# The entry to the last stage of a backward pass: one more block turned on TensorE, four row transfers moved to GpSimd's queue, new places for the stage's tiles

## The chip, the cores and the metric

The kernel runs on one core of one Trainium2 chip. Five engines work side by side, each with its own instruction stream: TensorE (PE, matrix products and transposes), VectorE (DVE), ScalarE (ACT), GpSimd (POOL) and SyncE (SP, which here only starts transfers). Transfers between HBM and SBUF, or inside SBUF, are done by 16 DMA engines; an engine's instruction stream only issues them. The metric is device time in microseconds (us) for one execution. The median over three runs is 2489.8 us.

## The reference

The reference is the forward pass of one transformer block and its gradients:

```
h = layernorm(x) * (1 + ca) + sa
x = x + ga * attention(h, wqkv, wo)          # 32 heads of 16, S = 2048, D = 512
h = layernorm(x) * (1 + cb) + sb
x = x + gb * (square(relu(h @ w1 + b1)) @ w2 + b2)
(sa, ca, ga, sb, cb, gb) = split(silu(c) @ w_mod, 6)
out, vjp = jax.vjp(f, x, wqkv, wo, w1, b1, w2, b2, c, w_mod); grads = vjp(grad_out)
```

Outputs are the block's result and the gradients of x, wqkv, wo, w1, b1, w2, b2, c and w_mod, all in bf16.

## The kernel before

The forward pass and the gradients of the dense part take the first 1,100 us or so. What matters here are the two last stages.

**The attention gradient** (lines 1541 to 1774) treats the 32 heads as eight head groups (`hg`) of four. One *unit* is one tile of 128 queries against 512 keys for the four heads of a group; there are NU = 512 of them. For each unit, TensorE makes the scores (`score`), ACT the exponentials (`expo`), TensorE the products with the upstream gradient and DVE the score gradients `dS_u` (`dp_pair`). Four units with neighbouring query tiles form a *block* `b`; there are 128. The gradient of Q needs `dS_u` turned, keys on partitions, and the turned data of a block is gathered in one tile, `dsT`, of which there are three in rotation. There are two ways to turn a unit:

- by a transposing DMA that SP issues (`transpose_unit`; line 1631 turns two units at once, line 1629 a single one);
- by 16 TensorE transposes (`pe_turn`, eight to a half, into the PSUM tile `ptT`) and a copy out of PSUM (token `T`, line 1760).

In even blocks all four units go by DMA, in two transfers of two. In odd blocks units 0 and 1 go together by DMA (line 1631), unit 2 alone by DMA (line 1629) and unit 3 over TensorE. Then `dq_quad` (line 1681, 16 matrix products for a block into the PSUM tile `dqacc`) and `dq_out` follow: ACT scales the result into `dqtmp` (line 1694) and POOL adds it to `dQacc` (line 1699); in the last round over the keys the sum goes to `dQst` in bf16. Two lists of tokens, `order_t` and `order_n`, fix by hand the order of instructions on PE, ACT, DVE, SP and POOL. `dq_out` of block b stands two blocks after its scores, so that the last two blocks' Q gradients are finished behind the last score.

**The last stage** (lines 1776 to 1959) takes the gradients of Q (`dq`, four slices of 128 rows) and of K and V (`vk`, eight slices), each slice 128 rows by 2048 tokens, and makes from them

- `dh1`: for each of 16 token tiles, 12 matrix products with `wT` (line 1858) into `pdh1`, then the layer norm's backward on DVE and ACT (lines 1862 to 1883) with `x0J` and `dx1J`, and the gradient of x;
- row sums of the same tiles (line 1877);
- `dwqkv`: 12 blocks of the weight gradient (`b` = 0 for Q, 1 and 2 for K and V; four `ic` each), 16 matrix products each with `h1J` (line 1892), then one or two copies out of PSUM and a store; beside them the gradients of w_mod and c (`wmod_grad`, `c_grad`, `c_out`).

`dwqkv` needs `dq` and `vk` with tokens on partitions, so at the stage's start every slice is turned by TensorE (line 1918, 24 groups of eight transposes) and copied to `dq_tok` or `dvk_tok` by DVE (line 1924) or ACT (line 1926), in the order of the list `order`.

Some of the slices are in SBUF at that point. Five are not: SP loads four (line 1778) into the buffers of the head group just finished and half of a fifth (line 1779), then `wT` (line 1781, 1.5 MB), and then copies the last head group's Q gradient from `dQst` into the other half of that fifth slice with four transfers of 16 rows (line 1783). Then come `x0J` and `dx1J` (lines 1792 and 1794, two token tiles to a transfer) and `sums_bc` (line 1799, 1.5 MB written). All of these stand on SP's one queue, in this order, and each waits where it stands. The transfers of that queue signal on eight semaphores in turn, so an issue can also wait for the transfer eight places ahead of it.

The stage's tiles are in a pool `big`, whose space is handed out in the order of allocation and lies over the buffers of the stage before. A tile's first writer therefore waits for the last user of what lay there. `wT` and the small tile `nb1` (line 1786, the first instruction of the stage on DVE) lie over the `dsT` tile of the last block and wait for its `dq_quad`.

At the end of `dwqkv`, step 9 of 0 to 11 calls `c_out`: two small DVE instructions form `dc` (lines 1837 and 1838), TensorE turns it (line 1840), ACT copies it and SP stores it. For `b` > 0, ACT copies one half of a weight block and DVE the other (lines 1903 and 1905), into one tile, and one transfer stores both (line 1907).

## Time and profile before

| what | value |
|---|---|
| median of three runs (2485.82 to 2491.23) | 2489.8 us |
| the profiled execution's span | 2501.3 us |
| attention gradient's last score gradient on DVE ends | 2378.1 us |
| first product of `dh1` starts | 2404.5 us |
| first product of `dwqkv` starts | 2454.1 us |
| last product of `dwqkv` ends | 2497.6 us |
| PE busy over the span | 93% |
| ACT, DVE, POOL busy over the span | 92%, 73%, 20% |

Times are from the start of the span of one profiled execution. The profile names an instruction by engine, line and operation with output and inputs; "idle before" is how long the engine stood still in front of it and what ended that. SPq is SP's instruction stream: its duration is that of issuing a transfer, not of the transfer. PE runs at a granted clock that the profile gives as a share of full speed. A wait for several things is put down to the one that came last by the profile; which one that is has at times to be worked out.

### The profile page before, as it was taken

The numbers are of one execution on the slowest core, as the hardware profiler recorded it, in microseconds if no ns is written. First come the engines' busy times: TensorE is split into PE (matmuls) and PEld (weight loads), VectorE is DVE, ScalarE is ACT, GpSimd is POOL, SyncE is SP. The second block draws the span as 40 slices with busy tenths as digits, with TensorE's granted clock in tenths as the row PEclk, the third lists the DMA queues.
The fourth block names the chain that finished last, engine by engine and source line by source line (L and its number), as shares of the span: only waits on it lengthen the run. The fifth ranks groups of instructions, "written<-read, shape, count | busy, mean of one in ns | idle before, by whom it ended". The sixth has DMA issues, their size and how long they took to land.

```text
span 2501.3 us, 49888 instructions
## 1 busy us (share of the span) xinstructions
PE 2324.0 (93%) x18948; PEld 783.4 (31%) x19036; DVE 1837.7 (73%) x2377; ACT 2303.7 (92%) x3560; POOL 488.0 (20%) x661
## 2 busy tenths in 40 slices
PE   8899899989998998999999999999999999999989
PEld 3232233223332333443223323233232323332344
DVE  6555354455435444579989999999999999999965
ACT  7999999999998999539999999999999999999944
POOL 2111223323533453110111101111011110110100
PEclk9999999999998999999999999999999999999999
DMA  4468463258546865979999999999999999999984
GB/s 146 130 167 176 144 150 97 88 166 142 98 95 142 151 131 110 256 200 196 201 192 206 199 198 202 196 204 203 205 205 198 205 202 199 200 198 214 201 253 133
DMA packets 1189503, 437.70 MB, mean 175 GB/s; under 512 B 1065867, under 2 KB 1160521, under 8 KB 1188878
## 3 DMA queue, kind: packets, MB, share of 16 engines
q1 hardware_dynamic: 1152414, 389.35, 79.0%
q0 software_dynamic: 19872, 27.09, 6.5%
q10 hardware_dynamic: 16976, 18.07, 2.9%
q8 instruction: 149, 2.44, 0.4%
q14 instruction: 92, 0.75, 0.1%
HBM read 98.30 MB, written 70.80 MB: 68 GB/s over the span
## 4 chain that ended last, share of the span: by engine, by line
ACT 40%; PE 38%; issue 8%; DVE 7%; DMA 3%; SPq 1%; ACTq 1%; POOL 0%; DVEq 0%; another core or an unknown queue 0%; POOLq 0%
ACT E_u L1600 24%; ACT ET L578 12%; PE dqacc L1681 4%; PE psST L576 3%; PE psS_A L1594 3%; PE accVK L1654 2%; PE pm L233 2%; ACT dsT L1760 2%; PE psS_B L1594 2%; PE pdh L1858 2%; PE oacc L592 2%; PE psS_C L1594 2%; PE pwq L1892 2%; PE pm L500 2%; PE pm L410 2%
## 5 line engine op out<-in xcount | busy, mean ns | idle before, releaser
L1616 DVE TENSOR_TENSOR dS_u<-psD_u,E_u 128x1024 bf16<-128x1024 f32 x1024 | 1185.9, 1218 | 77.1 <-PE psD_u L1614 30.2
L578 ACT ACTIVATE ET<-psST 128x1024 bf16<-128x1024 f32 x1024 | 941.9, 1242 | 16.6 <-PE psST L576 16.3
L1600 ACT ACTIVATE E_u<-psS_A 128x512 bf16<-128x512 f32 x768 | 509.9, 664 | 10.8 <-PE psS_C L1594 8.5
L1600 ACT ACTIVATE E_u<-psS_B 128x512 bf16<-128x512 f32 x768 | 503.2, 655 | 10.8 <-DMA dsT<-dS_u 2.7
L1614 PE MATMUL psD_u<-iv,ido 32*128 32x512 bf16 x2048 | 409.1, 388 | 1.5 <-DVE dS_u L1616 1.3
L576 PE MATMUL psST<-qt_sb,kt_sb 32*128 32x512 bf16 x2048 | 313.8, 386 | 48.0 <-ACT ET L578 41.0
L1600 ACT ACTIVATE E_u<-psS_C 128x512 bf16<-128x512 f32 x512 | 334.3, 653 | 3.1 <-PE psS_B L1594 1.1
L1594 PE MATMUL psS_B<-ik,iq 32*128 32x512 bf16 x768 | 296.1, 386 | 11.7 <-ACT E_u L1600 4.4
L1594 PE MATMUL psS_A<-ik,iq 32*128 32x512 bf16 x768 | 294.5, 383 | 11.0 <-DVE dwlast L237 1.0
L1699 POOL TENSOR_TENSOR dQacc<-dQacc,dqtmp 128x512 f32<-128x512 f32 x64 | 81.2, 1268 | 858.8 <-ACT dqtmp L1694 797.4
L1594 PEld LDWEIGHTS <-iq 32*128 32x128 bf16 x2048 | 129.7, 91 | 313.9 <-issue 296.9
L1654 PE MATMUL accVK<-dS_u,qz 128*32 128x512 bf16 x2048 | 213.5, 388 | 0.5 <-PE psD_u L1614 0.2
L592 PE MATMUL oacc<-ET,vaug 128*32 128x512 bf16 x2048 | 207.0, 394 | 3.9 <-DVE ostage L596 3.9
L1663 PE MATMUL accVK<-E_u,dOs_tok 128*16 128x512 bf16 x2048 | 204.5, 388 | 0.0
L1594 PE MATMUL psS_C<-ik,iq 32*128 32x512 bf16 x512 | 194.2, 379 | 4.5
L576 PEld LDWEIGHTS <-kt_sb 32*128 32x128 bf16 x2048 | 84.3, 91 | 328.2 <-issue 306.5
L1681 PE MATMUL dqacc<-dsT,KS_tok 128*32 128x512 bf16 x2048 | 145.7, 382 | 18.8 <-DMA dsT<-dS_u 5.0
L1760 ACT ACTIVATE dsT<-ptT 128x1024 bf16<-128x1024 bf16 x128 | 144.1, 1126 | 13.1 <-PE ptT L1644 12.2
L251 DVE COPY part<-pm 128x512 f32<-128x512 f32 (+2 forms) x106 | 65.2, 615 | 121.9 <-PE pm L233 111.8
L1614 PEld LDWEIGHTS <-ido 32*128 32x128 bf16 x2048 | 105.2, 91 | 101.3 <-issue 94.9
L1654 PEld LDWEIGHTS <-qz 128*32 128x32 bf16 x2048 | 58.5, 94 | 178.0 <-issue 162.9
L1699 POOL TENSOR_TENSOR dQst<-dQacc,dqtmp 128x512 bf16<-128x512 f32 x32 | 40.6, 1270 | 266.1 <-ACT dqtmp L1694 266.1
(415 smaller groups left out, 2688.7 us busy)
## 6 DMA issues: line engine op xcount, KB each, us to landing
p_st<-part POOLq DMA_DIRECT2D x36, 256.0 KB, 4.6
kt_sb<-qkT_st POOLq DMA_DIRECT2D x124, 64.0 KB, 3.0
wA<-in_B_w_dram SPq DMA_DIRECT2D x28, 256.0 KB
wB<-w1T_st SPq DMA_DIRECT2D x21, 256.0 KB
wA<-w2T_st SPq DMA_DIRECT2D x21, 256.0 KB
wB<-in_B_w_dram SPq DMA_DIRECT2D x21, 256.0 KB
p_st<-part POOLq DMA_DIRECT2D x28, 192.0 KB, 4.6
p_st<-part SPq DMA_DIRECT2D x18, 256.0 KB
```

The costliest lines, as they stand in the source:

```text
L576: PE.matmul(ps[:, hi, :], kt_sb[r:r + 32, kt * P:(kt + 1) * P], qt_sb[r:r + 32, :], start=True, stop=True, tile_position=(r, 0))
L578: ACT.activation(ET[:, 2 * pair:2 * pair + 2, :], ps[:], AF.Exp, scale=SCALE)
L592: PE.matmul(oacc[32 * hq:32 * hq + 32, :], lhsT, ET[:, hq, :], start=(kt == 0), stop=(kt == TT - 1), tile_position=(0, 32 * hq), skip_grou ...
L1594: PE.matmul(psS[:], st["q"][r:r + 32, qt * P:(qt + 1) * P], st["k"][r:r + 32, kc * 512:kc * 512 + 512], start=True, stop=True, tile_positi ...
L1600: ACT.activation(bst[u][0][:, hq, :], sst.pop((u, hq))[:], AF.Exp, scale=SCALE)
L1614: PE.matmul(psD[:, hi, :], st["do"][r:r + 32, qt * P:(qt + 1) * P], st["v"][r:r + 32, kc * 512:kc * 512 + 512], start=True, stop=True, til ...
L1616: DVE.tensor_tensor(dS_u[:, 2 * pair:2 * pair + 2, :], psD[:], E_u[:, 2 * pair:2 * pair + 2, :], ALU.mult)
L1654: PE.matmul(cur["vk"][32 * hq:32 * hq + 32, :], hst[hg]["qz"][:, qt, hq, :], bst[u][1][:, hq, :], start=(qt == 0), stop=False, tile_positi ...
L1663: PE.matmul(acc[32 * hq:32 * hq + DH, :], dOs_tok[:, qt, (hg * 4 + hq) * DH:(hg * 4 + hq + 1) * DH], E_u[:, hq, :], start=False, stop=(qt ...
L1681: PE.matmul(acc[32 * hq:32 * hq + 32, :], KS_tok[:, kc * 4 + kt, h * DH:h * DH + 32], tT[:, :, hq * 4 + kt, :], start=(kt == 0), stop=(kt ...
L1699: POOL.tensor_tensor(dst2, dst, tmp[:], ALU.add)
L1760: ACT.activation(dst, pt[:], AF.Identity)
```

## The change

The change touches the end of the attention gradient and the last stage.

- The third unit of the last block (unit 510) is turned by TensorE: `last_turn`, 16 more transposes into two PSUM banks that the scores had, each half copied by ACT. SP's single-unit transfer for it is dropped. The copies for unit 511 (token `T` of the last block) go from ACT to DVE.
- The four transfers `dQst` to `xs["dq", 3]` are issued by POOL and no longer by SP.
- `order` begins with the four slices of the idle head buffers and has ("vk", 6) later.
- `sums`, `dmod` are allocated ahead of `wT`, `dvk_tok` is two tiles of layout [4, TT, P] where it was one of [TT, HG, P], with the three `wmodJ` buffers as tiles of their own around them, `nb1` is allocated later, and its computation stands behind the transposes.
- The load of `sums` moves behind the loads of `x0J` and `dx1J` for six token tiles.
- `c_out` is split: `c_sum` (the two DVE instructions) stays at step 9 of `dwqkv`, the rest moves to step 10.
- For `b` > 0, the two halves of a weight block get a tile and a store each.

```
 def transpose_unit(u):
     if on_pe(u // 4) and qi >= 2:
-        if qi == 2:
+        if qi == 2 and u < NU - 2:
             SP.dma_start(out=dqt[u // 4][:, qi], in_=bst[u][1]..., transpose=True)
...
+def last_turn(half):
+    pt = psx.tile([P, 8, P], BF, name="ptL", tag=("ps0", "ps1")[half])
+    for i in range(8):
+        kt = i % 4
+        PE.transpose(pt[:, i, :], held["last"][:, 2 * half + i // 4, kt * P:(kt + 1) * P], identb[:])
+    ACT.activation(dqt[NU // 4 - 1][:, 2, 8 * half:8 * half + 8, :], pt[:], AF.Identity)
...
     elif c == "t" and 0 <= b - 1 < NU // 4:
+        if b == NU // 4:
+            last_turn(i - 1)
         pe_turn(b - 1, i - 1)
     elif c == "T" and 0 <= b - 1 < NU // 4:
         dst, pt = held.pop(i - 1)
-        ACT.activation(dst, pt[:], AF.Identity)
+        if b == NU // 4:
+            DVE.tensor_copy(dst, pt[:])
+        else:
+            ACT.activation(dst, pt[:], AF.Identity)
...
+sums = big.tile([P, 6, D], F32, name="sums_bc")
+dmod = big.tile([P, 6, D], BF, name="dmod_bc")
 wT = big.tile([P, 12, D], BF, name="wT_all")
 SP.dma_start(out=wT[:], in_=wT_st...)
 for h in range(4):
-    SP.dma_start(out=xs["dq", 3][64 + DH * h:64 + DH * h + DH, :], in_=dq_last[32 * h:32 * h + DH, :])
-order = (("vk", 6), ("vk", 0), ("vk", 1), ("vk", 2), ("vk", 3), ("dq", 0), ("vk", 7), ...)
-nb1 = big.tile([P, TT], F32, name="nb1")
-DVE.scalar_tensor_tensor(out=nb1[:], in0=mean1[:], scalar=-1.0, in1=rstd1[:], ...)
+    POOL.dma_start(out=xs["dq", 3][64 + DH * h:64 + DH * h + DH, :], in_=dq_last[32 * h:32 * h + DH, :])
+order = (("vk", 0), ("vk", 1), ("vk", 2), ("vk", 3), ("dq", 0), ("vk", 6), ("vk", 7), ...)
 load_x(0)
 load_x(1)
-sums = big.tile([P, 6, D], F32, name="sums_bc")
-SP.dma_start(out=sums[:], in_=rows_st[2:8, :]...)
-dmod = big.tile([P, 6, D], BF, name="dmod_bc")
+wmod_tile()
+wmod_tile()
+dvk_tok = [big.tile([P, 4, TT, P], BF, name=f"dvk_tok{i}") for i in range(2)]
+wmod_tile()
+nb1 = big.tile([P, TT], F32, name="nb1")
...
-PE.matmul(pw[:], h1J[:, t, ic * P:(ic + 1) * P], rhs[:, t, :], ...)
+PE.matmul(pw[:], h1J[:, t, ic * P:(ic + 1) * P], dq_tok[:, t, :] if b == 0 else dvk_tok[b - 1][:, :, t, :], ...)
...
     for i in range(2):
+        wblk = wk.tile([P, D], BF, name="wqblk", tag=("prod1", "dxn1")[i], bufs=3)
         ...
-    SP.dma_start(out=dst, in_=wblk.rearrange("p (v c) -> p v c", v=2))
+        SP.dma_start(out=rows[:, c0:c0 + 256], in_=wblk[:, 0:256])
...
+DVE.scalar_tensor_tensor(out=nb1[:], ...)          # behind the 24 groups of transposes
 norm_tile(0)
 for t in range(TT):
+    if t == 2:
+        SP.dma_start(out=sums[:], in_=rows_st[2:8, :]...)
...
     if i == 2 * DC + 1:
+        c_sum()
+    if i == 2 * DC + 2:
         c_out()
```

In the changed program, PE's order behind the last score is: `last_turn` and `pe_turn` by halves, the rest of the K and V products, `dq_quad` of block 126, ten transposes of the last stage, `dq_quad` of block 127, and then the other transposes. The first copy into `dvk_tok` on DVE and the load of `wT` both still wait for `dq_quad` of block 127, since they lie over its `dsT`.

More of the change, by code (lines that the diff above doesn't have):

```diff
@@ L1618, in dp_pair @@
                 held["dS"] = dS_u
+            if u == NU - 2:
+                held["last"] = dS_u
         def on_pe(b):
@@ L1782 @@
         for h in range(4):
-            SP.dma_start(out=xs["dq", 3][64 + DH * h:64 + DH * h + DH, :], in_=dq_last[32 * h:32 * h + DH, :])
-        order = (("vk", 6), ("vk", 0), ("vk", 1), ("vk", 2), ("vk", 3), ("dq", 0), ("vk", 7), ("dq", 1), ("vk", 4), ("dq", 2), ("vk", 5), ("dq", 3))
-        nb1 = big.tile([P, TT], F32, name="nb1")
-        DVE.scalar_tensor_tensor(out=nb1[:], in0=mean1[:], scalar=-1.0, in1=rstd1[:], op0=ALU.mult, op1=ALU.mult)
+            POOL.dma_start(out=xs["dq", 3][64 + DH * h:64 + DH * h + DH, :], in_=dq_last[32 * h:32 * h + DH, :])
+        order = (("vk", 0), ("vk", 1), ("vk", 2), ("vk", 3), ("dq", 0), ("vk", 6), ("vk", 7), ("dq", 1), ("vk", 4), ("dq", 2), ("vk", 5), ("dq", 3))
         x0s, dx1s = {}, {}
@@ L1797, with wmod_tile @@
         load_x(1)
-        sums = big.tile([P, 6, D], F32, name="sums_bc")
-        SP.dma_start(out=sums[:], in_=rows_st[2:8, :].unsqueeze(0).to_broadcast([P, 6, D]))
-        dmod = big.tile([P, 6, D], BF, name="dmod_bc")
-        wms = {}
+        wms, wtags = {}, ["wmodJ0", "wmodJ1", "wmodJ2"]
+        def wmod_tile():
+            wtags.append(wtags.pop(0))
+            return big.tile([P, 3 * D], BF, name="wmodJ", tag=wtags[-1], bufs=1)
+        wmod_tile()
[3 more added lines that the diff above has]
+        nb1 = big.tile([P, TT], F32, name="nb1")
         def load_wmod(k, h):
-            wms[k, h] = big.tile([P, 3 * D], BF, name="wmodJ", tag="wmodJ", bufs=3)
+            wms[k, h] = wmod_tile()
             SP.dma_start(out=wms[k, h][:], in_=w_mod[k * P:(k + 1) * P, 3 * D * h:3 * D * h + 3 * D])
@@ L1833, in c_grad, with c_sum, c_out @@
                                      scale=1.0, scalar=0.0, op0=ALU.mult, op1=ALU.add, accum_out=ccols[:, k, h:h + 1])
-        def c_out():
-            dc = wk.tile([P, 4], F32, name="dc", bufs=1)
+        dc = wk.tile([P, 4], F32, name="dc", bufs=1)
+        def c_sum():
             DVE.tensor_tensor(dc[:].unsqueeze(2), ccols[:, :, 0:1], ccols[:, :, 1:2], ALU.add)
             DVE.tensor_tensor(dc[:], dc[:], colc[:, 4:8], ALU.mult)
+        def c_out():
             pc = psd.tile([P, D], F32, name="pdc", tag="pdh1")
@@ L1845 @@
         dq_tok = dpool.tile([P, TT, D], BF, name="dq_tok", tag="dt")
-        dvk_tok = big.tile([P, TT, HG, P], BF, name="dvk_tok")
         xns = {}
@@ L1888, in dwqkv @@
         def dwqkv(b, ic):
-            rhs = dq_tok if b == 0 else dvk_tok[:, :, 4 * (b - 1):4 * b, :].rearrange("p t g c -> p t (g c)")
             pw = psw.tile([P, D], F32, name="pwq", tag="pw")
             for t in range(TT):
-                PE.matmul(pw[:], h1J[:, t, ic * P:(ic + 1) * P], rhs[:, t, :], start=(t == 0), stop=(t == TT - 1))
-            wblk = wk.tile([P, D], BF, name="wqblk", tag="prod1", bufs=3)
+                PE.matmul(pw[:], h1J[:, t, ic * P:(ic + 1) * P], dq_tok[:, t, :] if b == 0 else dvk_tok[b - 1][:, :, t, :], start=(t == 0), stop=(t == TT - 1))
             rows = out_2[ic * P:(ic + 1) * P, :]
             if b == 0:
+                wblk = wk.tile([P, D], BF, name="wqblk", tag="prod1", bufs=3)
                 ACT.activation(wblk[:], pw[:], AF.Identity)
@@ L1900, in dwqkv @@
                     srcv = pw.rearrange("p (g v d) -> p g v d", v=2, d=DH)[:, :, 1 - i, :]
-                    dstv = wblk[:, i * 256:(i + 1) * 256].rearrange("p (g d) -> p g d", d=DH)
+                    wblk = wk.tile([P, D], BF, name="wqblk", tag=("prod1", "dxn1")[i], bufs=3)
+                    dstv = wblk[:, 0:256].rearrange("p (g d) -> p g d", d=DH)
                     if i == 0:
@@ L1905, in dwqkv @@
                         DVE.tensor_copy(dstv, srcv)
-                dst = rows[:, D:3 * D].rearrange("p (v c) -> p v c", v=2)[:, :, (b - 1) * 256:b * 256]
-                SP.dma_start(out=dst, in_=wblk.rearrange("p (v c) -> p v c", v=2))
+                    c0 = D * (1 + i) + (b - 1) * 256
+                    SP.dma_start(out=rows[:, c0:c0 + 256], in_=wblk[:, 0:256])
         with tc.manual_schedule(engines={PE.engine, ACT.engine, DVE.engine}):
@@ L1921 @@
                     else:
-                        dst = dvk_tok[:, 8 * g:8 * g + 8, i, :]
+                        dst = dvk_tok[i // 4][:, i % 4, 8 * g:8 * g + 8, :]
                     if (2 * k + g) % 3 != 1:
@@ L1926 @@
                         ACT.activation(dst, pt[:], AF.Identity)
+            DVE.scalar_tensor_tensor(out=nb1[:], in0=mean1[:], scalar=-1.0, in1=rstd1[:], op0=ALU.mult, op1=ALU.mult)
             norm_tile(0)
@@ L1932 @@
                     load_x(t // 2 + 2)
+                if t == 2:
+                    SP.dma_start(out=sums[:], in_=rows_st[2:8, :].unsqueeze(0).to_broadcast([P, 6, D]))
                 if t in (4, 6, 7):
```

## The prediction

> **What bounds the kernel now.** I read the clock and span of the core, the chain of waits in order of time from 2376 us on, the timeline of each engine there, SP's own waits, stretches by engine and clock, and last the end. Up to 2376 us nothing is changed but line numbers; all that can move lies behind it. The chain first (start, duration, what):

> ```profile
> 2378.12 3.91 SPq L1631
> 2382.07 1.93 SPq L1629
> 2384.06 1.04 SPq L1778
> ...
> 2386.64 9.24 DMA qz<-dQc
> 2395.90 6.92 DMA x0J<-in_A_x_dram
> 2402.84 1.01 PE ptq L1918 x8
> ```

> From the last score gradient to PE's last transposes the chain is SP and transfers alone: SP is held by issuing two transposing DMAs, then loads follow. The last chain entry names x0J, but PE at 2402.84 transposes the slice `dq` 3, whose rows come by line 1783. The timeline (start, duration, instruction, idle before):

> ```profile
> 2386.60 1.17 PE L1681 MATMUL dqacc<-dsT,KS_tok 128*32 128x512 bf16 x16 [4.35 <-DMA dsT<-dS_u]
> 2387.84 0.38 SPq L1781 DMA_DIRECT2D wT_all<-wT_st  x1
> 2387.88 0.18 DVE L1786 SCALAR_TENSOR_TENSOR nb<-mean,rstd 128x16 f32<-128x16 f32 x1 [9.77 <-PE dqacc L1681]
> 2389.84 3.80 SPq L1783 DMA_DIRECT2D qz<-dQst  x4
> 2402.84 1.01 PE L1918 MATMUL ptq<-identb,qz 128*128 128x128 bf16 x8 [4.74 <-DMA x0J<-in_A_x_dram]
> 2404.50 0.63 PE L1858 MATMUL pdh<-wT_all,vkb 128*128 128x512 bf16 x1
> ```

> Everything waits for the last block's `dqacc` (4.35 us, for the single-unit transpose): wT's load, the first copies of DVE, and the rows of dQst. Those rows are issued behind wT on the same queue. SP's own waits say when wT was there:

> ```profile
> SPq L1794 <- DMA wT_all<-wT_st: 5.1, 1, 5.1
> SPq L1781 <- PE dqacc L1681: 0.5, 1, 0.5
> ```

> The 5.1 us ended at SP's issue at 2401.41, so wT landed at 2401.40; the trace's semaphore counts put the four row transfers at 2400.15 to 2402.38, the transpose of line 1631 at 2383.96 and that of line 1629 at 2386.47. So two arrivals a microsecond apart set the start of `dh1`: wT, then the rows, then 16 transposes (2402.84 to 2404.50). From there PE has no gap over a microsecond until step 9 of `dwqkv`:

> ```profile
> 2468.33 20.88 PE L1892 MATMUL pwq<-dvk_tok,h1J 128*128 128x512 bf16 x94
> 2490.41 0.27 PE L1840 MATMUL pdc<-identf,dc 128*4 128x128 f32 x1 [1.20 <-DVE dc L1838]
> 2490.52 7.07 PE L1892 MATMUL pwq<-dvk_tok,h1J 128*128 128x512 bf16 x31
> ```

> **The change part by part.**

> *SP without line 1629.* SP issues the first load at 2382.07 where it was 2384.06: 1.99 us earlier. Its waits (last scores at 2376.6, last K products at 2380.1) are over by then. What lands before `dqacc` of block 127 is now line 1631's transfer, 2383.96 against 2386.47: 2.51 us earlier.

> *The 16 transposes and the copies.* A group of eight takes 0.62 us on PE (line 1644), so 1.2 us more; out of the same stretch go 19 transposes of line 1918, by `order`, which ran there. ACT's copies 2 x 1.02 us (line 1760) are now those of unit 510, and DVE copies unit 511 after its last score gradient, at 2378.1: two copies of 0.69 (line 1924) with eight transposes between, done at about 2380.3, where ACT was done at 2380.43. `dqacc` of block 126 (2380.48, 1.05 us) does not move, and ends 2.4 us ahead of the landing. I cost this at nothing; the cover is that wait, and without it the 1.2 us would show.

> *`dqacc` of block 127* runs 2384.1 to 2385.2 (0.13 us after the landing, as before; before it ended at 2387.77). wT's issue follows at 2385.3, behind five loads whose issuing takes 2382.07 to 2384.65. POOL's sum (line 1699, 1.27 us from 2388.55) was done 2.05 us after `dqacc`: now 2387.2.

> *wT.* SP starts its loads 1.99 us earlier and the queue is free of line 1629's data 2.51 us earlier, so wT lands 2398.9 to 2399.4. Against that the rows, 0.26 MB, now go beside it: at the 241 GB/s of the stretch 2398.1 to 2402.8 at most 1.1 us. I take 2399.8 (bounds 2398.9 and 2400.5).

> *The rows on POOL's queue.* POOL has nothing behind them but the end of the program. Issues of 64 KB cost POOL 0.49 us in the median and 1.16 at most (line 188), so the last starts at about 2388.7 to 2390.7. The median time to landing (last number) over the run:

> ```profile
> kt_sb<-qkT_st POOLq DMA_DIRECT2D x124, 64.0 KB, 3.0
> ```

> and in the loaded stretch 918.5 to 924.5, with the load of SP's and ACT's queue above it:

> ```profile
> q1 hardware_dynamic: 1570, 1.88, 94.7%
> ...
> kt_sb<-qkT_st POOLq DMA_DIRECT2D x2, 64.0 KB, 4.1
> ```

> So 4.1 us beside a nearly full queue; the longest of 124 took 10.1. So the rows are there at 2392 to 2395, at worst about 2400.8. The 22 groups of transposes and copies ahead of them took 2387.97 to 2398.98, bound by the copies; from 2385.2 that ends near 2396.3, and the last slice is turned by 2397.5. All this is 2 us ahead of wT, which alone then sets the start of `dh1`: about 2399.9 for 2404.50, a gain of 4.6 us (bounds 5.5 and 3.9).

> *The clock.* PE's two waits cost half speed afterwards (stretch, length, busy us by engine, clock, DMA share, GB/s):

> ```profile
> 2398.10:2402.80 4.70, 0.00 (x1) 0.00 (x0) 0.88 (x2) 0.17 (x1) 0.00 (x0) 0.81 1.03 241
> 2402.80:2408.00 5.20, 4.94 (x24) 2.97 (x26) 0.69 (x1) 2.43 (x3) 0.00 (x0) 0.51 0.93 349
> ```

> The half clock lasted until 2407.9, so 3.4 us of `dh1` ran at half speed and lost 1.7 us. Afterwards PE would idle some 2.4 us ahead of wT. In this trace the idle times of 2.3 us (764.6, 1776.0) and 2.85 us (792.2) were each followed by half clock too, in stretches of 3.41 or 6.83 us. I take the same 1.7 us, so no difference; bounds 1.7 us gained (no half clock) and 1.7 lost (6.83 us of it). [...]

> *c_sum and c_out.* PE's last product before the stall started at 2468.33 + 20.88 - 0.38 = 2488.83; the pitch is 0.216 us, so the next was due at 2489.05 and came at 2490.52: 1.47 us. With `dc` ready a step earlier only the transpose's 0.11 us (2490.41 to 2490.52) stays: 1.4 us gained. The DVE instructions follow the same copy as before and now have 3.4 us of cover. Bounds 1.2 (the stall alone) and 1.5.

> *Stores of halves, layouts, `order`, sums, `nb1`.* The last store goes out after DVE's half either way; it is half as large, and ACT's half is issued (0.38 us) while DVE copies (0.42). I take 0.1 us gained, bounds 0.4 lost (an issue in the way) and 0.3 gained. A product reading `dvk_tok` in four pieces has the shape of `dqacc`'s reads of dsT, 382 ns against 388 for whole rows: nothing. `nb1` (0.18 us) is needed only by `norm_tile` once x0J is there, and x0J is next behind wT. Sums, first used at 2457, lands by 2415.

> Sum: 4.6 + 0 + 1.4 + 0.1 = 6.1 us; span 2501.3 to 2495.2. The profiled span lies 11.5 us over the median of the runs; the stages are the same, so I take the gain off the median: 2489.8 - 6.1 = 2483.7.

> **Rivals.**

> *The rows come last (15%).* DVE copies back to back from 2385.3 to 2396.3, and POOL must prepare its transfers in that time. If it could do so only afterwards, the last would be issued at 2397.8 and land 4.1 us later; 0.46 us and 16 transposes (1.66) give `dh1` at 2404.0, gain 0.5 + 1.5: 2487.8. Against it: of 124 issues of this size none took over 1.16 us, in a part of the run where DVE was 30 to 70% busy, with copies out of PSUM among its work. [...]

> *Warm entry (12%).* wT finds PE at full clock: 1.7 us more, 2482.0.

> *wT comes no earlier (6%).* If the 16 engines, not the issues, set 2401.40, only the rows' way is shortened: `dh1` at 2401.5, gain 3.0 + 1.5: 2485.3. For it: the engines are 97% busy or more from 2386.6 to 2402.8. Against: 2.5 us of transposing data leave that queue.

> *Slower (7%).* POOL's queue is served only when SP's is empty. SP now puts wT, six x0J and dx1J and sums in front: 2.4 + 1.6 + 1.6 + 1.6 = 7.1 MB from 2384 at 263 to 300 GB/s, done at 2408 to 2411. The rows land then, `dh1` starts 2.1 us later at 2410 to 2413, and 6 to 8 us lost against 1.5 gained give 2494 to 2497. It decides from a landing after 2403.9 on. Against it is the 4.1 us at 94.7% load.

> **How the numbers follow.** My forecast has 60%, with a range of its own of 2481.5 to 2486 from the bounds above. The predicted time is 2483.7. With the rivals and some 2 us for the median of few runs I give 2480.5 to 2489.5. A measurement of this kernel tells about 0.2% (5 us) from no change, so 2484.8 is the edge: of the forecast three quarters lie below it and of the warm entry nearly all, with a little of the others 0.57 faster; 0.35 the same; 0.08 slower.

> **What would show it.** SP's first load at 2382.1; `dqacc` of block 127 at 2384.1; POOL's four transfers landed by 2395 and the last transposes done by 2398 without a wait over a microsecond; `dh1` waiting for wT and starting near 2399.9; half clock for some 3.4 us of it; no idle PE at line 1864. It is wrong if `dq` 3 is the slice that PE waits for, or if wT lands later than 2401.

## The result, and the profile after

The changed kernel took 2482.47 us (median of 22 runs, 2471.86 to 2493.62), the kernel before 2490.35 us (22 runs, 2478.20 to 2499.89). The ratio is 0.9968, its 95% interval 0.9954 to 0.9981: some 7.9 us, a third of a per cent, faster. The forecast was 2483.7.

The profiled executions differ by more: 2501.3 us before, 2482.6 after. The last score gradient on DVE, ahead of which only line numbers changed, ended at 2378.11 before and at 2367.11 after. So 11.0 of the 18.7 us are no work of the change (the last section says what goes with part of them), and 7.7 us lie behind that point. From here on, times called *marks* are counted from the end of the last score gradient.

The chain of waits after (start, duration, what) answers to the chain of before:

```profile
2366.00 8.22 DMA dsT<-dS_u
2374.22 0.04 issue
2374.27 1.86 PE dqacc L1690 x16
2376.13 0.02 SPq L1797
...
2376.18 12.50 DMA wT_all<-wT_st
2388.68 0.05 issue
2388.73 0.39 PE pdh L1881
```

But for 0.02 us ahead of wT, SP's issuing no longer stands in it. What stands there is the last transposing transfer, `dqacc` of block 127, wT's load and `dh1`. The timeline after (start, duration, instruction, idle before and who ended it):

```profile
2370.93 0.58 SPq L1792 DMA_DIRECT2D iq<-dQc  x1
...
2374.27 1.84 PE L1690 MATMUL dqacc<-dsT,KS_tok 128*32 128x512 bf16 x16 [3.31 <-DMA dsT<-dS_u]
...
2376.18 0.38 SPq L1797 DMA_DIRECT2D wT_all<-wT_st  x1
...
2378.45 2.07 POOL L1799 DMA_DIRECT2D qz<-dQst  x4 [0.30 <-POOL dQst L1708]
...
2387.29 0.61 PE L1941 MATMUL ptq<-identb,qz 128*128 128x128 bf16 x8 [1.05 <-DVE dvk_tok L1947]
...
2388.73 0.39 PE L1881 MATMUL pdh<-wT_all,iq 128*128 128x512 bf16 x1 [0.38 <-DMA wT_all<-wT_st]
```

`dh1` waits for wT, as forecast, but only by 0.38 us. PE's wait ahead of slice `dq` 3 shrank from 4.74 to 1.05 us. Its releaser is named as a DVE copy; by the trace's semaphore counts the last row landed at 2387.04, and the transposes followed 0.25 us later, as they did behind the last row's landing of before. From the issue to that landing the rows took longer than forecast (DMA issues from 2374 to 2390; KB each, median us to landing):

```profile
qz<-dQst POOLq DMA_DIRECT2D x4, 64.0 KB, 7.1
```

The stretches by engine after (stretch, length, busy us of PE, its loads, DVE, ACT, POOL, granted clock, DMA share, GB/s) show the clock:

```profile
2374.20:2376.20 2.00, 1.93 (x18) 0.63 (x19) 0.00 (x0) 0.00 (x0) 0.00 (x0) 0.54 1.02 367
2376.20:2386.20 10.00, 10.00 (x165) 9.87 (x163) 8.79 (x14) 7.56 (x8) 3.34 (x5) 0.92 1.08 279
2386.20:2388.70 2.50, 1.09 (x17) 0.91 (x16) 1.24 (x3) 0.97 (x2) 0.00 (x0) 1.00 1.04 327
2388.70:2393.90 5.20, 5.12 (x23) 2.37 (x25) 2.03 (x7) 2.20 (x4) 0.00 (x0) 1.00 1.08 414
```

`dqacc` of block 127 fell into half clock (1.84 us for what took 1.17 before), but `dh1` starts at full clock, where before 3.4 us of it ran at half. At the end the stall of `pdc` is gone, and two stores follow ACT's and DVE's copies:

```profile
2450.90 24.34 PE L1914 MATMUL pwq<-dvk_tok,h1J 128*128 128x512 bf16 x112
2475.07 0.27 PE L1864 MATMUL pdc<-identf,dc 128*4 128x128 f32 x1
2475.18 3.62 PE L1914 MATMUL pwq<-dvk_tok,h1J 128*128 128x512 bf16 x16
...
2478.88 0.38 ACT L1926 ACTIVATE wqblk<-pwq 128x256 bf16<-128x256 f32 x1 [3.03 <-issue]
2479.29 0.81 SPq L1930 DMA_DIRECT2D out_dram<-wqblk  x2
```

The 7.7 us, stage by stage (all from the two timelines; landings from the semaphore counts, by which the last row of before landed at 2402.60, where the forecast had read 2402.38):

| mark or length, us | before | after | gain |
|---|---|---|---|
| SP's first load | 5.95 | 3.81 | 2.1 |
| `dqacc` of block 127 ends | 9.67 | 8.99 | 0.7 |
| wT landed | 23.29 | 21.57 | 1.7 |
| last row landed | 24.49 | 19.93 | 4.6 |
| first product of `dh1` | 26.40 | 21.61 | 4.8 |
| `dh1`, first product to first of `dwqkv` | 49.59 | 47.92 | 1.7 |
| `dwqkv`, first start to last end | 43.50 | 42.14 | 1.4 |
| from there to the end | 3.71 | 3.80 | -0.1 |
| end | 123.19 | 115.48 | 7.7 |

### The profile page after: what moved, and what is told of

It is laid out like the page before. It is cut to its first block, busy times and chain, and to the rows that moved or that the text cites. A ratio compares the mean times of both kernels' runs of the same rounds, so it can differ in the third digit from the quotient of the medians.

```text
span 2482.6 us, 49937 instructions
## 1 busy us (share of the span) xinstructions
PE 2319.5 (93%) x18967; PEld 782.2 (32%) x19052; DVE 1838.7 (74%) x2379; ACT 2302.5 (93%) x3560; POOL 491.3 (20%) x665
## 4 chain that ended last, share of the span: by engine, by line
ACT 40%; PE 38%; issue 8%; DVE 7%; DMA 4%; ACTq 1%; POOL 0%; SPq 0%; DVEq 0%; another core or an unknown queue 0%; POOLq 0%
ACT E_u L1600 24%; ACT ET L578 12%; PE dqacc L1690 4%; PE psST L576 3%; PE psS_A L1594 3%; DMA dsT<-dS_u 2%; ACT dsT L1774 2%; PE accVK L1663 2%; PE pm L233 2%; PE oacc L592 2%; PE psS_B L1594 2%; PE pdh L1881 2%; PE pm L424 2%; PE pm L500 2%; PE pm L410 2%
```

## The experiments

The change falls into five parts: A, unit 510 turned on TensorE; B, the rows on GpSimd's queue; C, places, order of slices, `nb1` and the sums; D, `c_sum` and `c_out`; E, two stores for a block. All marks stand in one table, each row from one profiled execution; "load to dh1" is the distance from SP's first load to the first product of `dh1`. SP's place relative to DVE drifts by up to 3 us from execution to execution (last section), so that distance compares better across kernels than the mark itself, though it scatters by over a microsecond too (e3). For e11 and e12, whose later loads waited for their buffers, it says nothing. The single times of e1 to e10 lie within the scatter of before and after and are not used.

| kernel | SP's first load | wT landed | last row | first `dh1` | load to dh1 | `dh1` | `dwqkv` | end |
|---|---|---|---|---|---|---|---|---|
| before | 5.95 | 23.29 | 24.49 | 26.40 | 20.45 | 49.59 | 43.50 | 123.19 |
| after | 3.81 | 21.57 | 19.93 | 21.61 | 17.80 | 47.92 | 42.14 | 115.48 |
| e1 after without A | 6.24 | 23.74 | 21.46 | 23.79 | 17.55 | 47.93 | 42.14 | 117.59 |
| e2 after without B | 4.26 | 18.69 | 20.56 | 21.70 | 17.44 | 47.91 | 42.14 | 115.32 |
| e3 before, PE kept busy | 6.93 | 23.04 | 23.97 | 25.63 | 18.70 | 47.91 | 43.51 | 120.76 |
| e4 after, DVE still | 2.51 | 19.06 | 17.57 | 23.41 | 20.90 | 47.91 | 42.14 | 117.27 |
| e5 before with A | 1.45 | 17.38 | 18.36 | 19.61 | 18.16 | 49.48 | 43.51 | 116.36 |
| e6 before with B | 6.25 | 24.56 | 22.03 | 24.61 | 18.36 | 49.49 | 43.51 | 121.56 |
| e7 after without D | 2.60 | 19.03 | 18.54 | 20.36 | 17.76 | 48.89 | 43.51 | 116.53 |
| e8 after without E | 2.92 | 19.66 | 19.17 | 20.30 | 17.38 | 47.91 | 42.14 | 114.37 |
| e9 rows by ScalarE | 1.40 | 18.13 | 19.04 | 20.07 | 18.67 | 47.91 | 42.14 | 113.69 |
| e10 `dqacc` warm | 3.58 | 20.53 | 19.31 | 20.57 | 16.99 | 47.93 | 42.14 | 114.44 |
| e11 last block on PE | -1.81 | 14.57 | 18.26 | 19.40 | 21.21 | 47.91 | 42.14 | 113.32 |
| e12 e11, rows on SP | -2.12 | 15.54 | 17.18 | 18.27 | 20.39 | 47.91 | 42.14 | 111.96 |

**e1: A undone.**

```diff
-                if qi == 2 and u < NU - 2:
+                if qi == 2:
...
-                        if b == NU // 4:
-                            last_turn(i - 1)
...
-                        if b == NU // 4:
-                            DVE.tensor_copy(dst, pt[:])
-                        else:
-                            ACT.activation(dst, pt[:], AF.Identity)
+                        ACT.activation(dst, pt[:], AF.Identity)
```

> The changed kernel with unit 510 turned by SP's transposing DMA again; all else as changed. Times run from the end of the last score gradient on DVE (changed kernel: SP's first load issued at 3.8 us, wT and the rows landed at 20.0 and 19.9, first product of dh1 at 21.6; kernel before: 5.9, 23.3, 24.3, 26.4). Theory 1 (SP's time and the transposing data bound the entry): first load at 5.9, first product of dh1 at 23.6 to 24.1. Theory 2 (moving the rows off SP's queue is what shortened the entry, the extra turn does little): first product at 21.6 to 22.3.

`dh1` started at 23.79, 2.2 us behind the changed kernel and 2.6 ahead of before; SP's first load came at 6.24. From that load on nothing is lost (17.55 against 17.80). So beside B, what A gives is SP's earlier start, as theory 1 has it. (The 20.0 us that the expectation names for wT of the changed kernel is when its first parts had landed; the last landed at 21.57, as in the table.)

**e2: B undone.**

```diff
-            POOL.dma_start(out=xs["dq", 3][64 + DH * h:64 + DH * h + DH, :], in_=dq_last[32 * h:32 * h + DH, :])
+            SP.dma_start(out=xs["dq", 3][64 + DH * h:64 + DH * h + DH, :], in_=dq_last[32 * h:32 * h + DH, :])
```

> The changed kernel with the four dQst rows issued by SP again, behind wT. Theory 1: wT lands at 19 to 20 us after the last score gradient, the rows within 1 us behind it as before, first product of dh1 at 21.5 to 22.5: the queue of the rows is worth less than 1 us. Theory 2: the rows land at 23 or later and dh1 starts at 24.5 to 25.5.

`dh1` at 21.70 against 21.61: B shows no worth here, as theory 1 has it, though wT and the rows lay outside the times that it named for them. The reason stands in the landings. With the rows behind it on its own queue wT was there at 18.69, 14.4 us after the first load, with the rows beside it only at 21.57, 17.8 us after; the rows then come last, at 20.56. The timeline of this kernel shows the order turned round: PE waits 0.20 us for the rows, none for wT:

```profile
2382.59 0.61 PE L1941 MATMUL ptq<-identb,qz 128*128 128x128 bf16 x8 [0.20 <-DMA qz<-dQst]
2383.03 0.61 PE L1941 MATMUL ptd<-identb,qz 128*128 128x128 bf16 x8
2383.48 0.38 PE L1881 MATMUL pdh<-wT_all,iq 128*128 128x512 bf16 x1
```

**e3: before, with 20 products that nobody reads, ahead of `dq` 3's transposes, so that PE doesn't idle there.**

```diff
+                if k == 11:
+                    warm = psw.tile([P, D], F32, name="warmJ", tag="pw")
+                    for _ in range(20):
+                        PE.matmul(warm[:], ones_bf[:], identb.unsqueeze(1).to_broadcast([P, 4, P]), start=True, stop=True)
```

> The kernel before with 20 idle matrix products of 512 columns (into a PSUM tile that nothing reads) on PE ahead of the last slice's turn, where PE waited 4.74 us. Theory clock (the 1.67 us that dh1 became shorter by, 49.59 to 47.92 us from its first product to the first of dwqkv, is the half clock that PE no longer enters): 47.9 us from first product of dh1 to first of dwqkv, the 16 transposes in 0.9 us instead of 1.66, no half clock between 22 and 30 us after the last score gradient. Rival (the first tiles wait for x0J or DVE, and sums' later load frees them): 49.6 us stays, with the clock full.

`dh1` took 47.91 us, to a hundredth what it takes in the changed kernel, and the stretches of this kernel show full clock across its entry (2387.82), where before had half for 6.83 us from 2401.05 on:

```profile
2385.00:2388.41 3.41, 3.41 (x29) 2.06 (x28) 0.39 (x1) 0.84 (x1) 0.00 (x0) 1.00 1.01 331
2388.41:2391.80 3.39, 3.39 (x18) 1.56 (x16) 1.24 (x4) 1.59 (x3) 0.00 (x0) 1.00 0.95 365
```

So the 1.67 us that `dh1` lost in the table of before and after are the clock alone.

This kernel shows one thing more. Its transfers are those of before, and yet `dh1` came 18.70 us behind SP's first load and not 20.45. Timeline of e3:

```profile
2386.93 0.61 PE L1922 MATMUL ptq<-identb,qz 128*128 128x128 bf16 x8
2387.37 0.61 PE L1922 MATMUL ptd<-identb,qz 128*128 128x128 bf16 x8
2387.82 0.38 PE L1858 MATMUL pdh<-wT_all,vkb 128*128 128x512 bf16 x1
```

The 16 transposes of `dq` 3 took 0.89 us at full clock for 1.66 at half, and the extra products held them up by 0.5 us. The rest is the landings: counted from the first load, the last row came at 17.04 for 18.54 and wT at 16.11 for 17.34. So such distances differ by over a microsecond between two profiles without any change in the transfers.

**e4: DVE kept still while GpSimd sends the rows** (the copies of the slices up to the 14th group on ACT).

```diff
-                    if (2 * k + g) % 3 != 1:
+                    if 2 * k + g > 13 and (2 * k + g) % 3 != 1:
```

> The changed kernel with the first 14 copies of turned slices all on ACT, so that DVE is idle while POOL issues the rows; dh1 starts later by the longer copies. What is read is the time from POOL's first row issue to the first packet of POOL's queue: 5.07 us in the changed kernel. Theory a (DVE's copies hold up GpSimd's preparation of the transfers): about 2.9 us, as around 162 us into the span of the kernel before. Theory b (the rows' packets wait in the DMA engines behind what SP has already handed over): 5 us stays.

From GpSimd's first issue (mark 9.27) to the first packet of its queue 5.01 us passed with DVE still, 5.07 in the changed kernel with DVE copying. So DVE's copies of the slices don't hold the rows up here (other copies were not tried): the hold-up that the first rival supposed does not show. `dh1` came late (23.41) since ACT alone copied.

**e5 and e6: before, with A alone and with B alone** (the same edits as in the change, nothing else of it).

> Kernel: before, with only its unit 510 turned on TensorE (SP's transpose of line 1629 dropped, the copies of unit 511 on VectorE); rows still on SyncE behind wT, all tiles, loads and stores as before. Times are counted from the end of the last score gradient on DVE. Theory 1 (the new places, the order of slices, the later sums and nb1 of the change are worth nothing at this stage; the turned unit alone takes 2.9 us of transposing data and 2 us of issuing out of wT's and the rows' way, and either it or the rows' new queue would do): first pdh at 21.2 to 22.2, as in the changed kernel with its rows on SyncE (21.70). Theory 2 (the new places and the order carry 2 us or more of the gain, since the changed kernel without the turned unit starts dh1 at 23.8 where before has 26.4): first pdh at 23.6 to 24.6. dwqkv stays at 43.5 in both, as c_out is not moved.

> Kernel: before, with only the four dQst rows issued by GpSimd instead of SyncE. Theory 1 (the rows' queue alone is what the changed kernel without the turned unit gained): wT lands at 23 to 24.4 as in before (23.29) or later by the rows' 0.26 MB, the rows land ahead of it at 20.5 to 22.5, and the first pdh comes at 23.5 to 24.5 instead of 26.4. Theory 2 (what that kernel gained comes from the new places, the order and the later sums): first pdh at 25.8 to 26.8.

e5 started `dh1` at 19.61, earlier than either theory had it, because SP was 2.4 us ahead of where it stood in the changed kernel; from the first load it took 18.16 us, 0.4 more than the changed kernel and 2.3 less than before. e6 started at 24.61, with wT at 24.56 as its last arrival: B alone took the rows out of the end, and started `dh1` 1.8 us ahead of before and 1.0 ahead of e3. It was 0.1 over theory 1's bound and far from theory 2's 25.8. From the first load on, A alone (18.16), B alone (18.36), A and B with the rest (17.80) and neither (18.70 in e3) lie no further apart than before and e3, whose transfers are the same. What stands out of that scatter is SP's earlier first load, which A brings; the 0.7 us between e5 and e2 that could be C's do not.

**e7: D undone** (`c_sum` called beside `c_out` at step 9).

```diff
                         c_sum()
-                    if i == 2 * DC + 2:
                         c_out()
```

> Kernel: the changed one, with c_sum and c_out both at step 9 again, as in before; c_sum keeps its place. Theory 1 (the stall of PE's transpose waiting for dc is all that moving c_out took away): the stretch from the first to the last pwq product is 43.4 to 43.6 us instead of 42.14, and PE idles 1.1 to 1.3 us ahead of pdc. Theory 2 (the split of dvk_tok or the two stores made those 1.35 us): 42.1 to 42.4.

43.51 us for `dwqkv`, and the stall is back in the timeline of this kernel:

```profile
2472.65 0.27 PE L1864 MATMUL pdc<-identf,dc 128*4 128x128 f32 x1 [1.20 <-DVE dc L1860]
```

D is worth 1.37 us, all of that stage's gain.

**e8: E undone** (one tile and one store for both halves, as before).

> Kernel: the changed one, with one tile and one store per weight block again, as in before. Theory 1 (two stores are worth nothing, since the last one goes out after DVE's half either way): from the end of the last pwq product to the end of the span 3.55 to 3.85 us (the changed kernel: 3.80), dwqkv at 42.1. Theory 2 (the extra issue of the other half is in the way of the last store): 3.3 to 3.5 us. Theory 3 (halving the store shortens the end): 3.95 to 4.2 us.

The end took 4.01 us, which fits theory 3 alone. Over all profiles it is 3.71, 3.72, 3.77, 3.95 and 4.01 with joined stores (before, e3, e5, e6, e8) and 3.56 to 3.86 with split ones: means of 3.83 and 3.73, a difference smaller than either spread. Whether E gives its 0.1 us stays open.

**e9: the rows by ScalarE's queue.**

```diff
-        for h in range(4):
-            POOL.dma_start(out=xs["dq", 3][64 + DH * h:64 + DH * h + DH, :], in_=dq_last[32 * h:32 * h + DH, :])
...
                         ACT.activation(dst, pt[:], AF.Identity)
+                        if 2 * k + g == 4:
+                            for h in range(4):
+                                ACT.dma_start(out=xs["dq", 3][64 + DH * h:64 + DH * h + DH, :], in_=dq_last[32 * h:32 * h + DH, :])
```

> Kernel: the changed one, with the four dQst rows issued by ScalarE (a queue that SyncE does not use) behind its second copy of the turned slices, instead of by GpSimd. With GpSimd five to six looks showed 4.7 to 5.4 us from the first row's issue to its first packet and 6.7 to 7.8 us from the last issue to the last landing. Theory a (that wait is the preparing of transfers that GpSimd's own queue needs): first packet 1 to 2.5 us behind ScalarE's first issue, last landing at most 4 us behind the last issue. Theory b (the 16 engines are taken by what SyncE has handed over before, whichever queue the rows come by): 4 to 6 us to the first packet and 6 to 8 us to the landing, as with GpSimd. In both wT lands within 1.5 us of where it did beside GpSimd's rows (17.0 to 17.8 us behind SyncE's first load), so dh1 gains at most 1 us.

First issue at 8.06, first packet at 13.0 (4.9 us), last issue at 11.78, last landing at 19.04 (7.3 us): theory b. The wait is not peculiar to GpSimd's queue (5.07 us to the first packet in the changed kernel). That it comes from what SP has handed over was not tried by itself, but the trace of before fits it. There 22 issues of `kt_sb` on GpSimd's queue come over 12 us behind GpSimd's issue ahead of them. In 15 of them the 16 DMA engines were under 75% busy in the next 3 us, and the first packet came 1.2 to 1.5 us after the issue; in the seven at 86% or more it came after 1.9 to 4.0. The share alone doesn't tell how long: 1.9 us at 92%, 2.9 at 95%.

**e10: PE kept busy ahead of `dqacc` of block 127** (16 products of 128x512 into a bank that nobody reads).

> Kernel: the changed one, with 16 idle products of 128x512 on TensorE between the dqacc of blocks 126 and 127, where it waits for the transposing transfer; they write a bank that nothing reads. Theory 1 (a window of 3.41 us of the clock gate with 2 us or more without a product makes the next window half clock): no half clock from 0 to 12 us behind the last score gradient, dqacc of block 127 takes 1.0 to 1.1 us instead of 1.84. Theory 2 (half clock there does not come from the wait): half clock as in the changed kernel. If SyncE's wT load waits for dqacc alone, it is issued 0.08 us behind its end; dh1 starts 17.0 to 18.2 us behind SyncE's first load as in the looks before (17.4 to 18.2), since the transfers set it: no gain that shows.

`dqacc` took 1.05 us, without half clock. wT left 0.08 us behind it and landed at 20.53, 16.95 us behind the first load. That lies within the scatter (16.4 to 17.8 with A and rows on a second queue): no gain that shows. The half clock there did come from the wait, as theory 1 has it.

**e11: all four units of the last block on TensorE; e12: that, with the rows on SP again.** e11's edit, cut to its core, and e12's:

```diff
+            if u == NU - 3:
+                held["pair"] = cur["dS"]
...
-            elif qi % 2 == 1:
+            elif qi % 2 == 1 and u != NU - 3:
...
-                            last_turn(i - 1)
+                            for half in range(2):
+                                last_turn(held["pair"][:, i - 1], i - 1, half, act_copy)
...
+                            if i == 2:
+                                for half in range(2):
+                                    last_turn(held["last"], 2, half, DVE.tensor_copy)
```

```diff
-            POOL.dma_start(out=xs["dq", 3][64 + DH * h:64 + DH * h + DH, :], in_=dq_last[32 * h:32 * h + DH, :])
+            SP.dma_start(out=xs["dq", 3][64 + DH * h:64 + DH * h + DH, :], in_=dq_last[32 * h:32 * h + DH, :])
```

> Kernel: the changed one, with all four units of the last block turned on TensorE: the pair of units 508 and 509 too (32 more transposes, four more copies, on ScalarE; those of unit 510 go to VectorE), and SyncE's last transposing transfer of two units dropped. Theory 1 (SyncE's lag decides: it is busy issuing transposing transfers without a break in the last 30 us, its first load came 1.5 to 4.3 us behind the last score gradient in the six kernels with the turned unit, and dh1 followed 17.4 to 18.2 us behind that load): first load at 1.8 to 2.3 us, where the last K products free its buffer; dqacc of block 127 ends at 7 to 8 us, held by TensorE's own work; without 0.5 MB of transposing data ahead wT lands 13 to 15 us behind the first load, and dh1 starts at 18 to 19.5 us behind the last score gradient (before 26.4, changed kernel 21.6); ratio to before 0.994 to 0.9965. Theory 2 (TensorE's 2.5 us of transposes are on the path that sets the end, since it also has the other slices to turn): last score gradient delayed or the other slices finished later, dh1 at 20 to 22, ratio 0.9965 to 0.998.

> Kernel: the one of the run before (all four units of the last block turned on TensorE), with the four dQst rows issued by SyncE behind wT again instead of by GpSimd. There wT had landed at 14.57 us and the rows only at 18.26, 6.8 us behind their last issue, while the other slices were turned by 16.95. Theory 1 (rows on a second queue share the engines with all that SyncE has handed over, and rows on SyncE's own queue come right behind wT): rows land within 2 us of wT, at 15 to 17 us; the last slice is turned without a wait over 0.5 us, and dh1 starts at 17.6 to 18.6 us (19.40 with GpSimd's rows). Theory 2 (any transfer of 64 KB needs 6 to 8 us from its issue there, whatever its queue): rows at 18 to 20 us, dh1 at 19 to 21. Time to before: 0.9955 to 0.998 by theory 1, 0.9965 to 0.999 by theory 2; the runs scatter by 0.2% each, so the trace tells them apart and the times hardly do.

e11 took 2482.89 us beside 2486.49 of before (ratio 0.9981, 0.9968 to 0.9995). The score gradients kept their pitch of 1.13 us, `dqacc` ended at 7.52 at full clock, and wT landed at 14.57. Its first load came even ahead of the last score gradient, at -1.81, not at 1.8: the buffer was free earlier than assumed. Yet `dh1` started only at 19.40, because now the rows on GpSimd's queue were last by 3.7 us. That start fits theory 1; the ratio lies far above that theory's range and just above the other's. Timeline of e11:

```profile
2385.89 0.61 PE L1950 MATMUL ptd<-identb,ido 128*128 128x128 bf16 x8
2388.06 0.61 PE L1950 MATMUL ptq<-identb,qz 128*128 128x128 bf16 x8 [1.56 <-DMA qz<-dQst]
2388.51 0.61 PE L1950 MATMUL ptd<-identb,qz 128*128 128x128 bf16 x8
2388.95 0.38 PE L1890 MATMUL pdh<-wT_all,iq 128*128 128x512 bf16 x1
```

With the rows behind wT on SP's queue again (e12) they landed at 17.18, 1.6 us behind wT, and that wait is all but gone. Timeline of e12:

```profile
2385.03 0.38 SPq L1806 DMA_DIRECT2D wT_all<-wT_st  x1
...
2387.03 2.48 SPq L1808 DMA_DIRECT2D qz<-dQst  x4
...
2394.81 0.61 PE L1950 MATMUL ptq<-identb,qz 128*128 128x128 bf16 x8 [0.43 <-DVE dvk_tok L1956]
2395.25 0.61 PE L1950 MATMUL ptd<-identb,qz 128*128 128x128 bf16 x8
2395.70 0.38 PE L1890 MATMUL pdh<-wT_all,iq 128*128 128x512 bf16 x1
```

`dh1` starts at 18.27, as theory 1 has it, though the rows came 0.2 us later than it allowed. Part of what the rows gained wT lost: it landed at 15.54 for e11's 14.57. The end, 111.96, is the earliest of all, 3.5 us ahead of the changed kernel's. The times can't confirm it: 2483.48 us beside 2489.69 of before, ratio 0.9974 (0.9959 to 0.9990), an interval that overlaps with the changed kernel's.

## Why the prediction was right, and which of its steps were not

The forecast's mechanism held in its main parts: the transposing transfer and SP's issue of it go, wT is the last arrival, `dh1` starts 4.8 us earlier (forecast 4.6), `c_out`'s stall goes. The sum was 6.1 us; behind the last score gradient it was 7.7, of which 1.67 came from a rival.

That the 4.8 lie so near the 4.6 is in part luck. SP's earlier first load accounts for 2.1 of them (e1) and the transposes at full clock for 0.8 (e3). The rest, some 1.9 us, lies in when the two arrivals come and which is last, and there the one profile of before is a late one: e3, with the same transfers, had its last row 1.5 us earlier from the first load on. Beside e3, the changed kernel ends 5.3 us earlier.

Of the signs that the prediction named, the first load, wT's landing, `dh1` waiting for wT and PE's missing stall at line 1864 came true. `dqacc` of block 127, the rows, transposes without a wait over a microsecond and the half clock in `dh1` did not. And `dq` 3 was a slice that PE waited for, 1.05 us, longer than for wT: by the first of its own signs of being wrong, that step was wrong. By steps:

- *SP without line 1629.* First load forecast at mark 3.96, measured 3.81. Right.
- *`dqacc` of block 127.* The landing of the pair's transfer was taken as unchanged (5.85) and came at 7.10, and the products took 1.84 us instead of 1.05: end at 8.99 instead of 7.1. Two mis-sized terms. The products' part is the half clock (e10 shows 1.05 without). The landing: 15 of its 16 parts came at 5.42 to 5.54, one 1.6 us later, while the queue of instruction loads moved a 16 KB packet (5.03 to 5.92); the same stands in e4, e5 and e7 to e10. That the one causes the other was not tried; in e2, beside such a packet too, all 16 parts came at 7.4.
- *wT.* Forecast at 21.7, measured 21.57, though issued 1.9 us later than assumed: two misses that cancelled, as the load took 12.5 us from its issue where the forecast had 14.5. The bound counted 1.1 us for the rows beside it; with A, wT landed 14.4 and 15.9 us behind the first load with rows on SP (e2, e5) and 16.4 to 17.8 with rows on a second queue.
- *The rows on POOL's queue.* The step that failed. They were to land 4.1 us after the issue and 5 us ahead of wT; they took 7.0 (6.7 to 7.8 in all kernels that used that queue) and were 1.6 us ahead. The 4.1 was the median of two issues in a stretch at 94.7%, no stand-in for a queue into which SP had just put 4 MB; 13 of the 124 issues counted there had taken over 6 us. So the step "all this is 2 us ahead of wT, which alone sets the start" holds by a margin so thin that in e7 to e9 the rows and their transposes were last. And B moves nothing that shows: the later of the two arrivals came 16.3 to 18.5 us behind the first load with rows on SP (before, e2, e3, e5) and 16.4 to 18.3 with rows on another queue (after, e1, e4, e6 to e10).
- *The clock.* Taken as no difference; 1.67 us gained. "Warm entry", given 12%, is what happened. The forecast had PE idle for 2.4 us ahead of wT; since the rows came late, its idling fell into two waits of 1.05 and 0.38 us. In the window of the clock's grid (last section) just ahead of the one in which `dh1` starts, PE idled 2.2 to 2.7 us in e5, e6 and e7, which entered at half clock, and at most 1.7 in ten others, which did not; before had been at half clock since a window with 2.9 us of idling, one further ahead. e7, which differs from the changed kernel by D alone, idled 2.30 there, so the warm entry is luck as well.
- *`c_sum`, `c_out`.* 1.4 forecast, 1.36 measured, 1.37 by e7. Right.
- *Stores, layouts, `order`, sums, `nb1`.* 0.1 gained was forecast, -0.1 measured; not to be told from nothing (e8). Nor is C: 0.7 us by e2 and e5, less than the scatter.

Of the rivals, "rows come last" came half true, and not by its mechanism: that DVE's copies keep POOL from its transfers was a supposition, and the first packet came 5.01 us after the issue with DVE still (e4), 4.9 by ScalarE's queue (e9), 5.07 in the changed kernel. "Slower" feared a queue served only when SP's is empty: a wait there was, 5.07 us to the first packet, but the landing came 6 us ahead of the point from which it would have decided (mark 25.8). "wT comes no earlier" did not happen: wT landed 1.7 us earlier, and with the rows behind it in e2 4.6 us earlier.

## What to carry to other kernels

When two arrivals a microsecond apart set a start, price them together: here, beside a deep queue, a second queue changed which of the two came last and not when, and what showed was SP's earlier first load. With less data ahead of them the rows did better on SP's own queue (landed at 17.18 in e12, at 18.26 on GpSimd's in e11). Read a transfer's time to landing from a stretch with the same data queued ahead, not from one with the same busy share: here it was 4.1 us in the stretch at 94.7%, and 7.0 behind SP's 4 MB. If a change is worth a third of a per cent and the unchanged part of the program scatters by more, fix an event at the border of the change and compare from there, and take a second profile of the kernel before: one alone can be a late one.

## What the runs showed of the hardware

```profile
2382.56:2385.97 3.41, 1.11 (x21) 0.96 (x19) 1.82 (x3) 1.02 (x1) 0.00 (x0) 1.00 1.06 281
2385.97:2389.38 3.41, 3.19 (x20) 2.19 (x20) 0.77 (x2) 1.88 (x3) 0.00 (x0) 0.50 1.10 393
```

```profile
2377.41:2380.82 3.41, 1.73 (x31) 1.55 (x28) 2.55 (x4) 1.57 (x2) 0.00 (x0) 1.00 1.08 210
2380.82:2384.23 3.41, 2.49 (x23) 1.71 (x25) 0.77 (x2) 1.61 (x2) 0.00 (x0) 1.00 1.08 363
```

*Half clock goes with most of the scatter.* Over the 14 profiles the end of the last score gradient (2358.9 to 2378.1 us) goes with the half-clock time ahead of it (37.5 to 92.2 us) at a correlation of 0.96, some 0.38 us for each. The profiled execution of before had 88.7 us of it, that of after 75.1. At 0.38 us for each that is 5 of the 11.0 us between them; the rest is not accounted for.

*SP lags behind DVE.* In the last 30 us ahead of the stage SP issued transposing transfers nearly without a break (0.05 to 0.10 us between two, in before and after); issuing one of two units took 4.8 to 6.0 us, one of a single unit 1.9 to 2.1 in those two. SP's lag moved the first load of kernels with A between 1.40 and 4.26, of those without between 5.95 and 6.93. The means differ by 3.5 us, of which SP's issue for unit 510 explains 1.9 to 3.2; whether the rest is chance was not settled.
